# One row block of w2 brought in as seven SyncE transfers and seventeen one-row GpSimd transfers

## The chip, the core and the metric

The kernel runs on one core of a Trainium2 chip. The metric is the time of one execution on the device in microseconds (us). Before the change the median of three runs is 344.36 us (344.31 to 344.41).

## What is computed

One decoding step for two sequences: an attention block with 32 heads and a cache of 4096 positions, beside a small feed-forward block, mixed by a gate. All tensors are bf16.

```python
x = A_x                                                 # 2 x 1 x 512
g = sigmoid((x * gate_w).sum(-1, keepdims=True))
q = (x @ wq)                                            # 512 x 4096, 32 heads of 128
p = softmax(einsum("bhqd,bhkd->bhqk", q, k_cache) * 128 ** -0.5)
a = einsum("bhqk,bhkd->bhqd", p, v_cache) as (2, 1, 4096) @ wo
b = relu(x @ w1) @ w2                                   # w1 512 x 1376, w2 1376 x 512
out = g * a + (1 - g) * b
```

The two caches are 64 MB each as the kernel reads them (2 x 32 x 4096 x 128 values of two bytes); with the weights the kernel reads 145.46 MB.

## The kernel before, in words

The kernel is written out by hand for five engines. Every instruction is put on a list of its engine by a call such as `pe(...)`, `dve(...)`, `sp(...)` or `pool(...)`. A call may name a marker that it raises (`signal`), markers of other engines that it waits for (`waits`), and transfer semaphores that it waits for (`dwaits`). `_Prog.emit` turns these into semaphore waits, in the order of the lists. A transfer's completion adds 16 to its semaphore.

All large inputs are issued by SyncE (SP) into one hardware queue, in this order: w1 and wq (lines 267 and 268), K in ten pieces (line 272), V in nine pieces (line 282), wo in two (lines 283 and 284), and w2 in six (lines 285 and 290). A K or V piece is issued when the buffer that it overwrites is free: `kv` holds five places of 4 MB.

- K stage: for each of 64 pieces VectorE turns K by transposes of 32 x 32 blocks (line 386) and TensorE multiplies it with padded queries (lines 197 and 407).
- Softmax (lines 413 to 432) is done once over all scores. The exponentials are laid out for the V stage by `spread(j)` (lines 444 to 448), in four copies of 32 partitions: two on GpSimd, one on VectorE, one on ScalarE. They raise `pt_{j}_0` to `pt_{j}_3`.
- V stage: nine jobs. `v_unit(j)` multiplies the weights with one V unit (line 461), `v_extract` (lines 467 and 471) picks out the diagonal blocks, and `o_gather` (line 486) collects the heads.
- The end: `project` multiplies with wo (line 508), `ffn_f(r)` multiplies the hidden row block r with w2's row block r (line 516), `wo_sum` adds wo's four partial sums into the same PSUM bank (line 540), and `ffn_last` (lines 202 and 208) does the last blocks. The program's order on TensorE there is: project, ffn_f(10), wo_sum, ffn_f(0) to ffn_f(7), half of ffn_f(8), ffn_last. Four copies (lines 579 and 581) bring the result to SBUF, and two transfers of one row each (line 293, from SyncE and ScalarE) take it out.

w2 lies in `kt`, the buffer of the turned K, over the exponentials that `spread` reads, so its transfers wait for the last spread (`pt_8_0` to `pt_8_3`). w2 has 1376 rows. Rows 0 to 1279 are laid out with ten consecutive rows on each partition, `w2[:, 0..9, :]`, and come as the column ranges w2b, w2c, w2d, w2e and w2f (768, 320, 64, 64 and 64 KB). The last 96 rows do not fill 128 partitions. Row block 10 therefore takes rows 1248 to 1375, one row of 512 values (1 KB) on each partition, and the hidden values that would count rows 1248 to 1279 twice are set to zero (line 379). This block is the transfer w2a, 128 KB, semaphore `w2a`, and `ffn_f(10, first=True)` waits for it at its first matmul:

```python
sp(lambda e: e.dma_start(w2[:, 10, :], B_w2[1248:1376, :]).then_inc(sem["w2a"], 16),
   waits=[f"pt_8_{hq}" for hq in range(4)])
...
dw = {10: [(sem["w2a"], 16)], 0: [(sem["w2b"], 16)], 6: [(sem["w2c"], 16)]}.get(r, [])
```

The five other pieces of w2 follow w2a in SyncE's list. GpSimd issues no transfer at all. ScalarE issues three small ones: x (two rows of 1 KB), gate_w (one row) and one row of the output. The first K and V stages bear on the change only through the queue that they fill; markers, engines and lines named above are all that the change and the steps below touch.

Of the kernel before, what the change touches and what calls it, by code (L numbers as in the profile page):

```python
# [85 lines left out]
def bass_gated_mix__gqa_block_cached__dense_activation_relu__decode_kernel(  # L86
# [54 lines left out]
    w1 = flat[:, 0:2752].bitcast(dt.bfloat16)  # L141
    E = flat[:, 0:2048].bitcast(dt.bfloat16)
    ET = flat[:, 4096:6144].bitcast(dt.bfloat16)
    w2f = flat[:, 0:2816].bitcast(dt.bfloat16)
    w2 = w2f.rearrange("p (r n) -> p r n", n=512)
# [8 lines left out]
    def psf(p0, p1, c0, n):  # L154
        return PSF[p0:p1, c0:c0 + n]
# [15 lines left out]

    for e in ("pe", "dve", "act", "pool"):
        P.sems[e] = nc.alloc_semaphore(e + "_ev")
    names = ["x", "gw", "wq", "w1", "wo0", "wo1", "w2a", "w2b", "w2c", "w2d", "w2e", "w2f", "out"]
    sem = {n: nc.alloc_semaphore("sem_" + n) for n in names}
    sem_k = [nc.alloc_semaphore(f"sem_k{s}") for s in range(3)]
    sem_v = [nc.alloc_semaphore(f"sem_v{s}") for s in range(4)]
# [10 lines left out]
    def adder(engine):  # L188
        def add(fn, waits=(), signal=None, dwaits=()):
            P.add(engine, fn, waits=[marker(w) for w in waits], signal=marker(signal) if signal else None, dwaits=dwaits)  # L190
        return add

    pool, dve, act, pe, sp = (adder(e) for e in ("pool", "dve", "act", "pe", "sp"))
# [12 lines left out]
    def held_at(e, out, lhsT, rhs, g, last):  # L206
# [9 lines left out]
         waits=["c_i16z"], signal="c_i16")  # L216
# [5 lines left out]
         waits=["c_i32z"], signal="c_i32")  # L222
# [6 lines left out]
         waits=["c_s4z"], signal="c_s4")  # L229
# [39 lines left out]
    for g, (u, halves) in enumerate(segments):  # L269
# [3 lines left out]
           waits=([f"kt_{last_of[g - 3]}"] if g >= 3 else ["pe_qr1"] if g == 2 else []))  # L273
    for j, (u, hf) in enumerate(jobs):
# [7 lines left out]
        sp(lambda e, dst=dst, src=src, s=s: e.dma_start(dst, src).then_inc(sem_v[s], 16), waits=[w])  # L282
    sp(lambda e: e.dma_start(wo_sb[:, 0:12288], wo_in[:, 0:12288]).then_inc(sem["wo0"], 16), waits=["pe_v_2"])
    sp(lambda e: e.dma_start(wo_sb[:, 12288:16384], wo_in[:, 12288:16384]).then_inc(sem["wo1"], 16))
    sp(lambda e: e.dma_start(w2[:, 10, :], B_w2[1248:1376, :]).then_inc(sem["w2a"], 16),
       waits=[f"pt_8_{hq}" for hq in range(4)])


    for name, c0, c1 in (("w2b", 0, 3072), ("w2c", 3072, 4352), ("w2d", 4608, 4864), ("w2e", 4352, 4608), ("w2f", 4864, 5120)):
# [145 lines left out]
    def spread(j):  # L435
        u, hf = jobs[j]
        f0, n = (2 * u, 2) if hf is None else (2 * u + hf, 1)
        src = ET.rearrange("p (k f e) -> p f k e", f=16, e=2)
        for hq in range(4):
            args = dict(out=ptm[32 * hq:32 * hq + 32, j % 2, 0:128 * n, hq, :].rearrange("p (f k) e -> p f k e", f=n),  # L440
                        in_=src[32 * hq:32 * hq + 32, f0:f0 + n])
            waits = ["dve_et3", "c_ptm"] + ([f"pe_v_{j - 2}"] if j >= 2 else [])
            if hq < 2:
                pool(lambda e, args=args: e.tensor_copy(**args), waits=waits, signal=f"pt_{j}_{hq}")  # L444
            elif hq == 2:
                dve(lambda e, args=args: e.tensor_copy(**args), waits=waits, signal=f"pt_{j}_{hq}")
            else:
                act(lambda e, args=args: e.activation(func=ACT.Copy, **args), waits=waits, signal=f"pt_{j}_{hq}")  # L448

    def v_unit(j):  # L450
        u, hf = jobs[j]
        at = region[:, u % 2, :] if hf is None else kv[:, (4, 2)[hf], :]
        rows = at.rearrange("p (m c d) -> p m c d", c=4, d=128)
        n = 64 if hf is None else 32
        for m in range(n):
            t = m % 4
            waits, dwaits = [], []
            if m == 0:
                waits = [f"pt_{j}_{hq}" for hq in range(4)] + ([f"dve_y{j - 2}"] if j >= 2 else [])
                dwaits = [(sem_v[u % 2], 16 * (u // 2 + 1)) if hf is None else (sem_v[2 + hf], 16)]  # L460
            pe(lambda e, m=m, t=t: e.matmul(  # L461
                psf(32 * t, 32 * t + 32, V_B[j % 2] * BANK, 512), lhsT=ptm[:, j % 2, 4 * m:4 * m + 4, :, :],
                rhs=rows[:, m], start=(m < 4), stop=(m >= n - 4), tile_position=(0, 32 * t)),
               waits=waits, dwaits=dwaits, signal=(f"pe_v_{j}" if m == n - 1 else None))

    def v_extract(u):
        dve(lambda e: e.tensor_tensor(out=Y.rearrange("p (c d) -> p c d", c=4),  # L467
                                      in0=psf(0, 128, V_B[u % 2] * BANK, 512).rearrange("p (c d) -> p c d", c=4),
                                      in1=maskc[:, :].unsqueeze(2).to_broadcast([128, 4, 128]), op=ALU.mult),
            waits=[f"pe_v_{u}", "dve_maskc"] + ([f"dve_x{u - 1}"] if u else []), signal=f"dve_y{u}")  # L470
        dve(lambda e: e.tensor_reduce(out=X2[:, u, :], in_=Y.rearrange("p (c d) -> p d c", c=4), axis=AX.X, op=ALU.add),  # L471
            waits=[f"dve_y{u}"], signal=f"dve_x{u}")
# [10 lines left out]
    def o_gather(b, js, start, stop):  # L483
        for j in js:
            u, first, last = jobs[j][0] % 4, start and j == js[0], stop and j == js[-1]
            pe(lambda e, u=u, j=j, first=first, last=last: e.matmul(  # L486
                psf(0, 32, O_C0, 128), lhsT=selx[:, 24 - 8 * u:56 - 8 * u], rhs=X2[:, j, :], start=first, stop=last),
               waits=[f"dve_x{j}"] + (["dve_rinv", "dve_selx"] if first else []) + (["dve_O0"] if b else []),
               signal=(f"pe_O{b}" if last else None))
        if not stop:  # L490
            return
        dve(lambda v, b=b: v.tensor_scalar(out=O_sb[:, b, :], in0=psf(0, 32, O_C0, 128), scalar1=rinv[:, b:b + 1],
                                           scalar2=gb[0:32, b:b + 1], op0=ALU.mult, op1=ALU.mult),
            waits=[f"pe_O{b}", "dve_rinv", "dve_g"], signal=f"dve_O{b}")
        for dq in range(4):
            pe(lambda e, dq=dq, b=b: e.matmul(psf(0, 128, R_C0 + 32 * b, 32), lhsT=s4[:, dq, :], rhs=O_sb[:, b, 32 * dq:32 * dq + 32],
                                              start=(dq == 0), stop=(dq == 3), tile_position=(0, 0)),
               waits=([f"dve_O{b}", "c_s4"] if dq == 0 else []), signal=(f"pe_R{b}" if dq == 3 else None))
        dve(lambda v, b=b: v.tensor_copy(out=oW[:, :, b], in_=psf(0, 128, R_C0 + 32 * b, 32)), waits=[f"pe_R{b}"], signal=f"dve_oW{b}")

    def fin(g):
        return psf(32 * g, 32 * g + 2, FIN_B * BANK, 128)

    def project():
        for r in range(32):
            dw = [(sem["wo0"], 16)] if r == 0 else [(sem["wo1"], 16)] if r == 24 else []
            t = r % 4
            pe(lambda e, r=r, t=t: e.matmul(psf(32 * t, 32 * t + 2, WO_B * BANK, 512), lhsT=oW[:, r, :], rhs=wo_sb[:, 512 * r:512 * r + 512],  # L508
                                            start=(r < 4), stop=(r >= 28), tile_position=(0, 32 * t)),
               dwaits=dw, waits=(["dve_oW0", "dve_oW1", "dve_z"] if r == 0 else []), signal=("pe_wo" if r == 31 else None))  # L510
        dve(lambda v: v.tensor_copy(out=YW, in_=psf(0, 128, WO_B * BANK, 512)), waits=["pe_wo"], signal="dve_yw")

    def ffn_f(r, first=False, groups=4):
        dw = {10: [(sem["w2a"], 16)], 0: [(sem["w2b"], 16)], 6: [(sem["w2c"], 16)]}.get(r, [])
        for g in range(groups):
            pe(lambda e, g=g: e.matmul(fin(g), lhsT=hT[:, r, :], rhs=w2[:, r, 128 * g:128 * g + 128],
                                       start=first, stop=False, tile_position=(0, 32 * g)),
               dwaits=(dw if g == 0 else []), waits=(["dve_h0", "dve_h1", "c_h10", "dve_z"] if first and g == 0 else []))
# [40 lines left out]
    for j in range(9):  # L559
        if j < 8:  # L560
            spread(j + 1)
        v_unit(j)
        v_extract(j)
        if j == 4:
            o_gather(0, [0, 1, 3], True, False)
        if j == 5:
            o_gather(0, [4], False, True)
    o_gather(1, [2, 5, 6, 7, 8], True, True)
    project()
    ffn_f(10, first=True)  # L570
    wo_sum()
    for r in range(8):
        ffn_f(r)
    ffn_f(8, groups=2)
    ffn_last()
    for c in range(4):
# [38 lines left out]
```

## Time and profile before

| what | value |
|---|---|
| runs, median (lowest to highest) | 344.36 us (344.31 to 344.41) |
| profiled execution, first to last instruction (span) | 342.9 us |
| difference of the median and the span | 1.46 us |
| DMA engines' share of the chain that ended last | 68% |
| read from HBM, mean rate over the span | 145.46 MB, 424 GB/s |
| share of SyncE's and ScalarE's hardware queues q1 and q10 | 98.5%, 0.0% |
| busy: TensorE, VectorE, ScalarE, GpSimd | 58%, 52%, 7%, 6% |
| w2's six transfers, issue to landing | 30.4 to 32.3 us |
| last w2 transfer's issue, SyncE held | 8.84 us |

The span is that of one execution under the profiler; the runs' times also hold what lies outside of the first and last instruction, so only differences are carried from one to the other. A busy share is an average over stages: TensorE is busy 58% of the time and yet waits for transfers at the end of the kernel. "Issue to landing" is the time from the instruction that starts a transfer to its completion, so it holds the time for which the transfer stands in the queue behind others. The trace also keeps one record for each DMA packet (queue, start, duration, bytes) and one for each semaphore increment of a transfer; a transfer that runs on several of the 16 DMA engines raises its semaphore once from each of them.

### The profile page before, as it was taken

What the parts mean: (1) busy time and instruction counts of PE and PEld (TensorE: products, weight loads), DVE (VectorE), ACT (ScalarE), POOL (GpSimd) and SP (SyncE); (2) the same over time, 40 slices, a digit from 0 to 9 for tenths busy, and PEclk for the clock granted to TensorE, in tenths of its full rate; (3) what the DMA queues carried; (4) which work ended last, traced back from release to release, by engine and by line L of the source; (5) the groups of instructions that cost most, each with busy time, mean ns of one, the idle gap of its engine ahead of it and who ended that gap; (6) DMA issues with size and microseconds to landing.
All of it is one profiled execution on the core that took longest, in us unless ns stands there. A gap on an engine that the chain in (4) does not pass through costs nothing.

```text
span 342.9 us, 2540 instructions
## 1 busy us (share of the span) xinstructions
PE 197.8 (58%) x1228; PEld 54.3 (16%) x972; DVE 178.5 (52%) x127; ACT 23.1 (7%) x71; POOL 19.9 (6%) x36
## 2 busy tenths in 40 slices
PE   0177329799969799699799337220706043150656
PEld 0141001111111111111111013100303011020231
DVE  2239059899789899698999562220100103020121
ACT  1040000000000000000000240000000000000000
POOL 8000000000000000000000040110100101000000
PEclk9999959989999999989999858755656756565787
DMA  8998989899998999999999999999999999998996
GB/s 348 428 489 369 482 375 482 382 474 413 438 489 367 429 443 466 392 459 390 475 420 436 461 390 420 445 466 413 443 413 445 428 428 443 413 468 382 440 401 239
DMA packets 4196, 145.61 MB, mean 425 GB/s; under 512 B 469, under 2 KB 986, under 8 KB 1242
## 3 DMA queue, kind: packets, MB, share of 16 engines
q1 hardware_dynamic: 4178, 145.46, 98.5%
q8 instruction: 8, 0.13, 0.2%
q14 instruction: 2, 0.02, 0.0%
q10 hardware_dynamic: 8, 0.00, 0.0%
HBM read 145.46 MB, written 0.00 MB: 424 GB/s over the span
## 4 chain that ended last, share of the span: by engine, by line
DMA 68%; DVE 15%; PE 13%; ACT 1%; issue 1%; POOL 0%; SPq 0%; DVEq 0%
DMA kv<-in_A_k_cache_dram 31%; DMA kv<-in_A_v_cache_dram 23%; DVE kt L386 13%; DMA kt<-in_B_w_dram 9%; PE PS L461 6%; DMA kv<-in_A_wq_dram 4%; PE PS L407 3%; PE PS L197 3%; ACT kt L428 1%; PE PS L333 1%; DVE mpad L413 1%; DVE kt L471 1%; POOL ptm L444 0%; DVE qbuf L467 0%; DVE kt L432 0%
## 5 line engine op out<-in xcount | busy, mean ns | idle before, releaser
L386 DVE STREAM_TRANSPOSE kt<-kv 128x2048 f32<-128x2048 f32 x64 | 141.2, 2274 | 22.4 <-DMA kv<-in_A_k_cache_dram 22.3
L407 PE MATMUL PS<-kt,qbuf 128*128 128x512 bf16 x256 | 105.7, 413 | 31.8 <-DVE kt L386 26.3
L197 PE MATMUL PS<-kt,qbuf 128*128 128x512 bf16 x256 | 105.1, 411 | 0.0
L461 PE MATMUL PS<-kv,ptm 128*32 128x512 bf16 x512 | 46.5, 541 | 79.0 <-DMA kv<-in_A_v_cache_dram 76.0
L467 DVE TENSOR_TENSOR qbuf<-PS,maskc 128x512 f32<-128x512 f32 x9 | 6.2, 692 | 109.0 <-PE PS L461 109.0
L407 PEld LDWEIGHTS PS<-kt,qbuf 128*128 128x128 bf16 x256 | 25.5, 100 | 139.9 <-DVE kt L386 72.7
L461 PEld LDWEIGHTS PS<-kv,ptm 128*32 128x32 bf16 x512 | 19.0, 129 | 105.1 <-issue 98.6
L444 POOL COPY ptm<-kt 32x512 bf16<-32x512 bf16 (+1 forms) x18 | 11.5, 638 | 268.7 <-DVE rsum L475 175.6
L360 ACT ACTIVATE qbuf<-PS 32x8 bf16<-32x8 bf16 x40 | 7.9, 196 | 134.2 <-PE PS L197 132.7
L448 ACT ACTIVATE ptm<-kt 32x512 bf16<-32x512 bf16 (+1 forms) x9 | 5.3, 603 | 100.1 <-PE PS L461 98.7
L471 DVE TENSOR_REDUCE kt<-qbuf 128x128 f32<-128x512 f32 x9 | 9.3, 1028 | 0.3
L428 ACT ACTIVATE kt<-PS,negm 128x512 bf16<-128x512 f32 x8 | 5.4, 696 | 30.4 <-DVE negm L424 30.4
L333 PE MATMUL PS<-kv,xTw 128*32 128x512 bf16 x32 | 3.6, 629 | 5.9 <-DMA kv<-in_A_wq_dram 5.9
L478 PE MATMUL PS<-rsum,sell 128*32 128x1 f32 x4 | 0.4, 196 | 10.1 <-DVE rsum L475 10.1
L432 DVE STREAM_TRANSPOSE kt<-kt 128x1024 bf16<-128x1024 bf16 x4 | 5.0, 1245 | 1.7 <-ACT kt L428 1.4
L348 DVE CAST qrow<-PS 128x256 bf16<-128x256 f32 x2 | 2.4, 1396 | 6.4 <-PE PS L333 6.4
L508 PE MATMUL PS<-kv,oW 128*2 128x512 bf16 x32 | 3.4, 590 | 1.4 <-DMA kv<-in_A_wo_dram 1.4
L300 PE MATMUL PS<-ident,x_sb 3*128 3x3 bf16 x4 | 0.3, 166 | 6.2 <-DMA x_sb<-in_gate_w_dram 6.2
L486 PE MATMUL PS<-kt,selx 128*32 128x128 f32 x18 | 3.4, 328 | 0.3 <-DVE kt L471 0.3
L303 DVE COPY xT<-PS 128x12 bf16<-128x12 bf16 x1 | 0.2, 169 | 6.5 <-PE PS L300 6.5
L230 POOL MEMSET ptm<- 128x4096 bf16 x1 | 3.5, 3501 | 0.0
L413 DVE TENSOR_REDUCE mpad<-PS 128x1 f32<-128x2048 f32 x1 | 2.3, 2290 | 2.1 <-PE PS L197 2.1
(64 smaller groups left out, 44.2 us busy)
## 6 DMA issues: line engine op xcount, KB each, us to landing
kv<-in_A_k_cache_dram SPq DMA_DIRECT2D x4, 4096.0 KB, 31.6
kv<-in_A_v_cache_dram SPq DMA_DIRECT2D x2, 4096.0 KB, 27.0
kv<-in_A_wq_dram SPq DMA_DIRECT2D x1, 4096.0 KB, 15.0
kv<-in_A_wo_dram SPq DMA_DIRECT2D x1, 3072.0 KB, 29.3
kt<-in_B_w_dram SPq DMA_DIRECT2D x1, 1376.0 KB, 5.8
kv<-in_A_wo_dram SPq DMA_DIRECT2D x1, 1024.0 KB, 31.3
kt<-in_B_w_dram SPq DMA_DIRECT2D x1, 768.0 KB, 31.9
kt<-in_B_w_dram SPq DMA_DIRECT2D x1, 320.0 KB, 32.3
```

What stands on the lines that cost most here:

```text
L197: return e.add_instruction(mybir.InstMatmult(start_tensor_calc=start, stop_tensor_calc=stop, tile_size=(128, 128), tile_position=(0, 0), l ...
L333: pe(lambda e, n=n, t=t: e.matmul(psf(32 * (n % 4), 32 * (n % 4) + 32, (QR_B + n // 4) * BANK, 512), lhsT=xTw[:, t, :], rhs=wq_sb[:, t, n ...
L360: act(lambda a, hq=hq: a.activation(out=qbuf[32 * hq:32 * hq + 32, g % 2, :, :, 32 + 32 * hq], in_=cols[32 * hq:32 * hq + 32, u4 // 2, 2 * ...
L386: dve(lambda v: v.transpose(out=dst, in_=pairs[:, h, 64 * rr:64 * rr + 64]), waits=([f"pe_sc_{i - NKT}"] if i >= NKT else ["pe_h"] if i == ...
L407: return e.matmul(args[0], lhsT=args[1], rhs=args[2], start=first, stop=last)
L413: dve(lambda v: v.tensor_reduce(out=mpad[:, 0:1], in_=psf(0, 128, 0, 2048), axis=AX.X, op=ALU.max), waits=["pe_sc_63", "c_mpad"], signal=" ...
L428: act(lambda a, bk=bk, e2=e2: a.activation(out=blocks[:, bk, :, 16 * e2:16 * e2 + 16], in_=psf(0, 128, bk * BANK, 512).rearrange("p (r n) ...
L444: pool(lambda e, args=args: e.tensor_copy(**args), waits=waits, signal=f"pt_{j}_{hq}")
L448: act(lambda e, args=args: e.activation(func=ACT.Copy, **args), waits=waits, signal=f"pt_{j}_{hq}")
L461: pe(lambda e, m=m, t=t: e.matmul(psf(32 * t, 32 * t + 32, V_B[j % 2] * BANK, 512), lhsT=ptm[:, j % 2, 4 * m:4 * m + 4, :, :], rhs=rows[:, ...
L467: dve(lambda e: e.tensor_tensor(out=Y.rearrange("p (c d) -> p c d", c=4), in0=psf(0, 128, V_B[u % 2] * BANK, 512).rearrange("p (c d) -> p ...
L471: dve(lambda e: e.tensor_reduce(out=X2[:, u, :], in_=Y.rearrange("p (c d) -> p d c", c=4), axis=AX.X, op=ALU.add), waits=[f"dve_y{u}"], si ...
```

## The change

Row block 10 of w2 no longer comes as one transfer of 128 rows. SyncE brings partitions 0 to 110 as seven transfers of 15, 14, 13, 9, 7, 5 and 48 rows, in the place of w2a and with its waits on the first of them, all on semaphore `w2a`. GpSimd brings partitions 111 to 127 as seventeen transfers of one row each on a new semaphore `w2s`; the first waits for the same four markers. The calls to the GpSimd list stand behind the last `spread`. `ffn_f(10)` waits for 7 x 16 = 112 on `w2a` and 17 x 16 = 272 on `w2s`.

```diff
-    names = ["x", "gw", "wq", "w1", "wo0", "wo1", "w2a", "w2b", "w2c", "w2d", "w2e", "w2f", "out"]
+    names = ["x", "gw", "wq", "w1", "wo0", "wo1", "w2a", "w2b", "w2c", "w2d", "w2e", "w2f", "w2s", "out"]
...
-    sp(lambda e: e.dma_start(w2[:, 10, :], B_w2[1248:1376, :]).then_inc(sem["w2a"], 16),
-       waits=[f"pt_8_{hq}" for hq in range(4)])
+    ready = [f"pt_8_{hq}" for hq in range(4)]
+    few, p0 = [], 0
+    for n in (15, 14, 13, 9, 7, 5, 48):
+        few.append((p0, p0 + n))
+        p0 += n
+    for p0, p1 in few:
+        sp(lambda e, p0=p0, p1=p1: e.dma_start(w2[p0:p1, 10, :], B_w2[1248 + p0:1248 + p1, :]).then_inc(sem["w2a"], 16),
+           waits=ready if p0 == 0 else [])
...
+    def w2_single():
+        for p in range(111, 128):
+            pool(lambda g, p=p: g.dma_start(w2[p:p + 1, 10, :], B_w2[1248 + p:1249 + p, :]).then_inc(sem["w2s"], 16), waits=ready if p == 111 else [])
...
-        dw = {10: [(sem["w2a"], 16)], 0: [(sem["w2b"], 16)], 6: [(sem["w2c"], 16)]}.get(r, [])
+        dw = {10: [(sem["w2a"], 112), (sem["w2s"], 272)], 0: [(sem["w2b"], 16)], 6: [(sem["w2c"], 16)]}.get(r, [])
...
+    w2_single()
     o_gather(1, [2, 5, 6, 7, 8], True, True)
```

## The prediction

> **What bounds the kernel now.** I read the chain of waits first, then busy time in short stretches of the tail, then SyncE's and TensorE's timelines. The chain, from the last softmax-weight copy on:
>
> ```profile
> 306.97 0.28 DVE ptm L446
> ...
> 307.33 0.33 SPq L285
> ...
> 307.70 0.43 SPq L290
> ...
> 308.17 32.26 DMA kt<-in_B_w_dram
> ...
> 340.47 0.33 PE PS L516 x10
> 340.80 0.44 PE PS L208 x6
> ...
> 341.27 0.28 DVE out_sb L579
> ```
>
> Columns: start, duration, what. Transfers into kt (w2) end the kernel; after the last pieces of w2 only 0.8 us of matmul, a copy and the output's trip are left. These 32 us are not w2's own: it is 1.4 MB behind 8 MB of wo and V in one queue. The stretches of the tail (length, busy time of PE, PEld, DVE, ACT, POOL, clock, share of the 16 DMA engines busy, GB/s):
>
> ```profile
> 317.00:327.00 10.00, 5.40 (x64) 2.28 (x64) 1.71 (x2) 0.00 (x0) 0.00 (x0) 0.77 1.00 429
> ...
> 338.00:339.00 1.00, 0.54 (x9) 0.00 (x0) 0.52 (x1) 0.00 (x0) 0.00 (x0) 0.67 0.92 340
> 339.00:340.00 1.00, 0.75 (x32) 0.42 (x32) 0.17 (x1) 0.00 (x0) 0.00 (x0) 1.00 0.56 203
> 340.00:341.00 1.00, 0.69 (x26) 0.28 (x16) 0.08 (x1) 0.08 (x1) 0.00 (x0) 1.00 0.21 59
> ```
>
> Full until 338, then 0.92, 0.56, 0.21: the engines do not finish together. The trace's landing records (one per engine and transfer) say how unevenly. w2f, the last piece, lands between 339.09 and 339.64 on seven engines, at 340.31 on one, and between 340.78 and 340.97 on eight. Mean 340.17, last 340.97: perfect balance would be worth 0.80 us, and the end is set by the eight late engines alone. I followed packets (each starts within some 10 ns of its engine's last). An engine falls behind by about 1.5 us when a 16384-byte packet of the instruction queue q8 runs on it (eight in the span, the last at 331.8, each on another engine).
>
> **What is removed and added.** The same 128 rows of 1 KB come. Prices from the packet records: a 1024-byte packet 46 ns, a semaphore increment (a 4-byte packet) 9 ns. w2a is now 8 rows and one increment on each engine: 8 x 46 + 9 = 377 ns.
>
> How are odd numbers of rows spread? Rows of the trace: gate_w, one row, made one packet and one increment; x, two rows, two of each; 128 rows, 8 packets on each of 16 engines. I extend this: n rows below 16 go to n engines, one each, 48 rows three to each, always from the same first engine. The first five engines then get 9 rows and 7 increments, 9 x 46 + 7 x 9 = 477, **+0.10 us**; the next two 8 and 6, +0.05; two 7 and 5, -0.01; four 6 and 4, -0.07; then -0.12 and -0.18; the last 3 rows and one increment, 147, **-0.23 us**. [...]
>
> The seventeen single rows add 46 + 9 = 55 ns to each engine if they go round, one engine getting two. Bounds: 0.055, and with all increments on all engines (below) 0.20.
>
> Which engines are late? Only one can be named: the engine that carried gate_w, so the first, is among the seven early ones. Eight of the other fifteen are late. Best case, the eight late ones are the relieved ones and the last is the most relieved: -0.23 + 0.055 = -0.18 us. Worst, a late one is among the first five and gets two singles: +0.10 + 0.20 + 0.05 = +0.35. One late engine among the four loaded ones that remain is enough to move the end the loaded way, so I take +0.10 + 0.055 = **+0.15 us**.
>
> **SyncE's queue.** It issues 6 transfers more ahead of w2b to w2f.
>
> ```profile
> 307.33 0.33 SPq L285 DMA_DIRECT2D kt<-in_B_w_dram  x1
> 307.70 10.74 SPq L290 DMA_DIRECT2D kt<-in_B_w_dram  x5
> 341.61 0.32 SPq L293 DMA_DIRECT2D out_dram<-out_sb  x1
> ```
>
> An issue takes 0.43, yet five took 10.74: the fifth, w2f, held SyncE 8.84 us, until 318.4, right after V unit 6 landed (317.83). It was the tenth transfer in flight. If that is a limit of nine, the n-th of now sixteen gets in when the (n-9)-th has landed. V unit 6, its successor, wo0 and wo1 land at 317.8, 327.5, 334.9, 337.4. The sixth short transfer goes in at 317.8, the seventh at 327.5, w2b at 335, w2c at 337.5, and w2d, w2e, w2f by their own 0.45 each, to 339.3. x's first packet started 0.4 us after its issue ended, so w2f is in the engines by 339.7. The late ones need it after w2e, landing 340.79; they work on w2c at 339.7. Cost on the late engines **0**; the early ones run dry for about a microsecond, covered by their 1.3 to 1.9 us of lead. If the limit counts packets instead, I get w2f in at 336.7: 0 as well. Without that cover, w2f's 1 us would be the price.
>
> **GpSimd and the new wait.** The singles wait for the four copies of the last spread, ready at 307.24; nothing is behind them on GpSimd. TensorE's line 516 waits for all of them at row block 10, with everything to the end queued behind:
>
> ```profile
> 338.21 0.32 PE L516 MATMUL PS<-kt,hT 128*2 128x128 bf16 x4
> 339.23 0.40 PE L540 MATMUL PS<-qbuf,selw 128*2 128x128 f32 x8 [0.69 <-DVE qbuf L511]
> 339.65 0.51 PE L516 MATMUL PS<-kt,hT 128*2 128x128 bf16 x24
> 340.47 0.33 PE L516 MATMUL PS<-kt,hT 128*2 128x128 bf16 x10 [0.32 <-DMA kt<-in_B_w_dram]
> ```
>
> Blocks 10, the wo sum and r = 0 to 5 are 0.32 + 0.40 + 0.51 = 1.23 us and must be over at 340.43, when w2c lands: the singles are free until 339.2. The only small transfer that met a full queue, gate_w, landed 4.5 us after its issue ended (1.55 to 6.03): its row went behind some seven queued packets, then one packet of the big queue, then its increment. So the last issue may end at 334.7, or (334.7 - 307.3) / 17 = **1.6 us each**. No GpSimd issue is in the trace; ACT's two took 0.55 and 0.23, SyncE's 0.33 to 0.43, and SyncE's longest was 8.84 when blocked. Ends: 17 x 0.23 = 4 us, hidden; 17 x 8.84 = 150 us, absurdly late. The nearest row is a small issue on an engine's own queue, 0.55: done at 317, cost **0**. [...]
>
> **Sum.** +0.15 in the queues, 0 elsewhere. The profiled span is 342.9 and 1.46 below the median of the runs, 344.36; I keep that difference: 343.05 + 1.46 = **344.5 us**.
>
> **Rivals.**
> *All increments on all engines* (0.24). Every single row then puts 17 increments, not one, on each engine: 17 x 9 + 46 = 0.20, the end +0.30, 344.7. For: nothing in the trace; against: gate_w and x post one increment per engine used. [...] The turns would still suffice: 7 packets ahead and 18 turns make 25, and an engine has 28 large packets left before w2a.
> *The late engines are the relieved ones* (0.07): down to -0.18, 344.2.
> *GpSimd is too slow* (0.14, the slower side): from 1.6 us per issue on, each 0.1 us more adds 1.7 us; at 2 us the last is issued at 341.3, lands at about 342.8, and 2 us of matmuls follow where they now end at 341.24: some 348. At 1.65 to 1.75, 345.3 to 347. Against it: every issue row but the blocked one is under 0.6.
> *The change doesn't spread as meant* (0.07): singles all on one late engine cost 17 x 55 = 0.94 there, less its relief or plus its load, 345.1 to 345.4; the 63 rows of the six odd transfers piled on one engine would make (63 + 3 - 8) x 46 ns = 2.67 there, of which the lead of an early one (1.3 to 1.9) hides half or more: 345.2 to 345.7.
> *SyncE's slots starve the late engines* (0.05): up to 1 us, 344.9 to 345.4; decides if w2c or w2f comes over 1.1 us later than worked out.
> *Faster by over 0.7* (0.05): would need nearly all of the 0.80; five rows less are 0.23. Only instruction packets falling on other engines could do it.
>
> **Chances.** A measurement of this kernel can tell about 0.2%, 0.69 us. My forecast has 0.38; with the first two rivals, all within 0.69, same is 0.69. Slower: 0.14 + 0.07 + 0.05 = 0.26. Faster 0.05. The forecast's own range is 344.2 to 344.7; the range 344.1 to 345.6 takes in the queue bounds (-0.18, +0.35), the spread and the slot rivals, and leaves out most of GpSimd's 0.14 and the 0.05.
>
> **What would show it.** w2f's landing about 0.15 later and the chain still ending in kt; GpSimd's issues under 1.6 us each and done by 334; line 516's first four matmuls still at about 338.2. Wrong if these wait for GpSimd's transfers, or if the share of busy DMA falls below 1 before 338.

## The result and the profile after

Five runs of the changed kernel have a median of 345.80 us (345.49 to 346.10), five of the kernel before 344.31 (344.21 to 344.41): 1.49 us slower by the medians, ratio 1.0041, 95% interval 1.0027 to 1.0054. The prediction was 344.5 us, range 344.1 to 345.6. The profiled execution has a span of 344.2 us; 342.9 before. These 1.3 us are what the traces can account for; the other 0.2 lies outside of the spans or between executions, and no run explains it.

The chain of waits of the changed kernel still ends in kt, as before (start, duration, what):

```profile
308.92 32.69 DMA kt<-in_B_w_dram
...
341.65 0.33 PE PS L526 x10
341.98 0.54 PE PS L208 x6
...
342.55 0.28 DVE out_sb L590
```

Compare with the chain before: the matmuls that wait for w2c begin at 341.65 instead of 340.47, 1.18 us later, and what follows takes 0.10 us longer. So the loss is in the transfers ahead of them: w2f's last landing is at 342.25 instead of 340.97, and the span ends 1.97 us after it, where it ended 1.98 us after it before. The stretches of the tail show in what form (length, busy time of PE, PEld, DVE, ACT, POOL, clock, share of the DMA engines busy, GB/s). First the kernel before, from 336 to 338:

```profile
336.00:337.00 1.00, 1.00 (x16) 0.29 (x8) 0.00 (x0) 0.00 (x0) 0.00 (x0) 0.50 0.96 383
337.00:338.00 1.00, 1.00 (x16) 0.24 (x12) 0.00 (x0) 0.00 (x0) 0.00 (x0) 0.50 1.02 404
```

and the changed kernel:

```profile
336.00:337.00 1.00, 1.00 (x16) 0.43 (x12) 0.00 (x0) 0.00 (x0) 0.00 (x0) 0.50 1.10 330
337.00:338.00 1.00, 0.95 (x12) 0.02 (x3) 0.00 (x0) 0.00 (x0) 0.00 (x0) 0.50 1.03 302
338.00:339.00 1.00, 0.64 (x8) 0.10 (x8) 0.00 (x0) 0.00 (x0) 0.00 (x0) 0.50 0.95 319
339.00:340.00 1.00, 0.52 (x8) 0.09 (x4) 0.65 (x1) 0.00 (x0) 0.00 (x0) 0.97 0.86 321
340.00:341.00 1.00, 0.59 (x24) 0.30 (x28) 0.04 (x1) 0.00 (x0) 0.00 (x0) 1.00 0.64 222
341.00:342.00 1.00, 0.66 (x36) 0.32 (x26) 0.00 (x0) 0.00 (x0) 0.00 (x0) 1.00 0.17 49
```

The engines stay busy about a microsecond longer, and they move less while busy: 319 GB/s at a share of 0.95, where a share of 0.92 moved 340 before, and 302 GB/s at 1.03 in the stretch from 337 to 338, where the kernel before moved 404 at 1.02. Smaller packets alone lower the rate too (in the kernel before 8192 bytes take 313 ns on average, 1024 bytes 46 and 512 bytes 27: 26, 22 and 19 bytes for each ns), so the packet records have to be asked: the packets that start from 336 to 337 and from 337 to 338 take 1.10 and 1.03 us of each engine, and at the mean duration that each size has in the kernel before they would take 0.84 and 0.80. So the engines are not idle, their packets are slow. The table of queues has a new line:

```profile
DMA packets 4786, 145.61 MB, mean 423 GB/s; under 512 B 1076, under 2 KB 1576, under 8 KB 1832
## 3 DMA queue, kind: packets, MB, share of 16 engines
q1 hardware_dynamic: 4224, 145.44, 98.4%
...
q0 software_dynamic: 544, 0.02, 0.1%
```

GpSimd's seventeen rows made 544 packets, not 34. By the packet records these are 272 of 64 bytes and 272 increments: each row is cut into 16 pieces with 16 increments, and 544 packets on 16 engines are 34 on each. The busy share of that queue, 0.1%, looks harmless.

What did not happen is in the timeline of GpSimd, SyncE and TensorE:

```profile
306.36 8.25 POOL L458 DMA_DIRECT2D kt<-in_B_w_dram  x17 [1.77 <-issue]
308.45 17.79 SPq L296 DMA_DIRECT2D kt<-in_B_w_dram  x5
...
339.68 0.23 PE L526 MATMUL PS<-kt,hT 128*2 128x128 bf16 x4 [0.39 <-DMA kt<-in_B_w_dram]
340.10 0.40 PE L550 MATMUL PS<-qbuf,selw 128*2 128x128 f32 x8 [0.19 <-DVE qbuf L521]
340.81 0.51 PE L526 MATMUL PS<-kt,hT 128*2 128x128 bf16 x24 [0.31 <-DMA kt<-in_B_w_dram]
```

GpSimd issued all seventeen in 8.25 us. Row block 10's matmuls start 1.5 us later than before, at 339.68, but block 10 and the wo sum are over at 340.50, before w2b lets the next matmuls start at 340.81: the new wait costs nothing. Nor is it GpSimd's rows that block 10 waits for. By the landing records these are there at 338.83, and the last of SyncE's seven transfers at 339.63.

### The profile page after: what moved, and what is told of

Same layout as the page of the kernel before. It is cut to its first block, busy times and chain, and to the rows that moved or that the text cites. A ratio compares the mean times of both kernels' runs of the same rounds, so it can differ in the third digit from the quotient of the medians.

```text
span 344.2 us, 2565 instructions
## 1 busy us (share of the span) xinstructions
PE 196.9 (57%) x1228; PEld 53.9 (16%) x972; DVE 178.1 (52%) x127; ACT 23.1 (7%) x71; POOL 28.2 (8%) x53
## 4 chain that ended last, share of the span: by engine, by line
DMA 76%; DVE 11%; PE 11%; SPq 1%; issue 0%; DVEq 0%
DMA kv<-in_A_k_cache_dram 31%; DMA kv<-in_A_v_cache_dram 31%; DVE kt L392 10%; DMA kt<-in_B_w_dram 9%; PE PS L471 5%; DMA kv<-in_A_wq_dram 4%; PE PS L413 3%; PE PS L197 2%; PE PS L339 1%; SPq L291 1%; DVE kt L481 0%; DVE qbuf L477 0%; PE PS L208 0%; SPq L296 0%; SPq L267 0%
## 5 line engine op out<-in xcount | busy, mean ns | idle before, releaser
L471 PE MATMUL PS<-kv,ptm 128*32 128x512 bf16 x512 | 44.4, 520 | 81.7 <-DMA kv<-in_A_v_cache_dram 80.5
L471 PEld LDWEIGHTS PS<-kv,ptm 128*32 128x32 bf16 x512 | 18.3, 124 | 106.3 <-issue 100.8
L458 POOL DMA_DIRECT2D kt<-in_B_w_dram x17 | 8.3, 494 | 1.8 <-issue 1.8
```

The source lines that it names most:

```text
L458: pool(lambda g, p=p: g.dma_start(w2[p:p + 1, 10, :], B_w2[1248 + p:1249 + p, :]).then_inc(sem["w2s"], 16), waits=ready if p == 111 else [])
L471: pe(lambda e, m=m, t=t: e.matmul(psf(32 * t, 32 * t + 32, V_B[j % 2] * BANK, 512), lhsT=ptm[:, j % 2, 4 * m:4 * m + 4, :, :], rhs=rows[:, ...
```

## The experiments

Each number is the difference of the medians against the kernel before on the same chip; the ratio has its 95% interval. In every trace but that of the thirty-four rows the span ends 1.97 to 2.11 us after w2f's last landing, at granted clocks between 0.50 and 1.00 from 340 to 341, so TensorE's part in these differences is at most 0.14 us. `ready` stands for the four markers `pt_8_0` to `pt_8_3`. In "added" runs the block comes as before in one transfer of 128 rows, and the named transfers are added, into a spare tile that nothing reads; TensorE's block 10 waits for them too. The others bring the same 128 rows of the block by other transfers.

**First round: which half of the change costs?**

SyncE's half alone. 

> Row block 10 comes from SyncE alone: the same 15, 14, 13, 9, 7, 5 and 48 rows, then 16 and 1 row instead of GpSimd's seventeen transfers; each has a semaphore of its own. Theory A (the seventeen one-row transfers cost the time, because the changed kernel's trace shows 272 packets of 64 bytes and 272 increments on GpSimd's queue, 34 packets on each DMA engine): +0.1 to +0.4 us against the kernel before, from 8 more increments of 9 ns and up to 2 more rows of 46 ns on the loaded engines. Theory B (the uneven split of SyncE's transfers costs it): +1.0 us or more.

```diff
+    for i, n in enumerate((15, 14, 13, 9, 7, 5, 48, 16, 1)):
+        sp(lambda e, p0=p0, n=n, i=i: e.dma_start(w2[p0:p0 + n, 10, :], B_w2[1248 + p0:1248 + p0 + n, :]).then_inc(sem["w2a%d" % i], 16),
+           waits=ready if i == 0 else [])
+        p0 += n
```

Measured: +0.60 us, 1.0020 (1.0011 to 1.0029). Between the two theories: neither half is the whole.

GpSimd's half with an even split. 

> SyncE brings 112 rows in one transfer, evenly, and GpSimd the last 16 as sixteen one-row transfers. Theory A: +0.8 to +1.1 us (16/17 of the 0.96 us by which the last landing of the second piece of wo, which lies ahead of row block 10 in the queue, is later in the changed kernel's trace). Theory B: under +0.3 us.

```diff
+    sp(... w2[0:112, 10, :] ..., waits=ready)
...
+        pool(lambda e, p0=p0, n=n: e.dma_start(w2[p0:p0 + n, 10, :], B_w2[1248 + p0:1248 + p0 + n, :]).then_inc(sem["w2s"], 16),
+             waits=ready if i == 0 else [])     # p0 from 112, n = 1, sixteen times
```

Measured: +1.19 us, 1.0035 (1.0023 to 1.0048). Near theory A, and yet A was wrong, as the next two show.

The 16 rows in one GpSimd transfer. 

> SyncE brings 112 rows in one transfer and GpSimd the last 16 rows in a single transfer. Theory A (it is the number of one-row transfers): a sixteenth of the cost of sixteen, so within 0.1 us of the kernel before. Theory C (that GpSimd issues a transfer at all, a third queue beside the others, costs it): +0.7 us or more.

Measured: +0.50 us, 1.0017 (1.0008 to 1.0026). Neither A nor, quite, C. The code is the excerpt above with one transfer of n = 16.

The 16 rows from ScalarE, one by one. 

> SyncE brings 112 rows in one transfer and ScalarE the last 16 as sixteen one-row transfers. x and gate_w made one packet of 1024 bytes and one increment for each row on ScalarE's queue. Theory A (the many small packets on all engines cost): 16 x 55 ns on the first engine alone, which is among the early ones, so within 0.1 us of the kernel before. Theory D (many transfers on another queue cost, however few packets they make): +0.7 us or more.

Measured: +0.61 us, 1.0018 (1.0009 to 1.0027). A had said that nothing would be lost, D +0.7 or more; neither holds. The code is the excerpt above with the sixteen calls on ScalarE's list. All three kernels with 112 rows in one SyncE transfer lose at least half a microsecond, whatever brings the other 16 rows. Something in the 112-row transfer itself costs time, although by its packets it is cheaper than the 128-row transfer (7 x 46 + 9 = 331 ns on an engine instead of 377, an estimate from the prices of the packet records).

The packet records show what. In the kernel before, a packet of wo's second part (8192 bytes) takes 313 ns on average and one of w2b (6144 bytes) 242. In the run with one GpSimd transfer these are 328 and 277, and the slow ones run between 335.2 and 337.8, while SyncE's 112 rows are in flight (335.0 to 337.3). The 8192-byte packets stand ahead of the rows in every engine's queue, so an engine is slowed there by rows that *other* engines carry. New theory, P: a row that an engine writes to partitions which another engine serves in full transfers collides with that engine's packets. That each engine has partitions of its own in full transfers is a part of the theory: no record here names an engine or the partitions that it writes. The pair of runs in the third round tests whether it matters where the rows go.

**Second round: number of transfers, or whose partitions?**

Eight transfers of 16 neighbouring rows. 

> SyncE alone brings the block as eight transfers of 16 neighbouring rows. By the packet prices it is 8 x (46 + 9) = 440 ns on each engine instead of 377, +0.06 us. Theory P (rows that an engine writes to partitions which other engines write in full transfers collide with those engines' packets: in the trace with one GpSimd transfer the 8192- and 6144-byte packets that run while the rows are in flight took 7.2 us more in all, 0.45 us per engine): +0.5 us or more, and at least 0.2 us more than the same with rows eight apart. Theory N (the number of transfers and increments): the same as with rows eight apart, and no slow 8192-byte packets.

```diff
+    for j in range(8):
+        sp(lambda e, j=j: e.dma_start(w2[16 * j:16 * j + 16, 10, :], B_w2[1248 + 16 * j:1264 + 16 * j, :]).then_inc(sem["w2a"], 16),
+           waits=ready if j == 0 else [])
```

Measured: +0.83 us, 1.0024 (1.0015 to 1.0033).

Eight transfers of rows eight apart. 

> As the one before, but each transfer takes rows eight apart, so that its 16 rows are spread over all partitions. Number of transfers, packets and increments are the same. Theory P: +0.1 to +0.4 us, the excess of the 8192- and 6144-byte packets under half of that with neighbouring rows. Theory N: the same time as with neighbouring rows.

```diff
+        sp(lambda e, j=j: e.dma_start(w2[j::8, 10, :], B_w2[1248 + j:1376:8, :]).then_inc(sem["w2a"], 16), ...
```

Measured: +0.79 us, 1.0020 (1.0011 to 1.0029). Spreading the rows did not help as P had said it would; the slow packets cost nearly as much (10.7 us of engine time in all, 11.8 with neighbouring rows). P had been read too simply: which of the 128 rows fall on partitions that their engine writes in full transfers is shown for neither kernel, so that fewer packets would be slow here was the author's guess. Nor is N right by itself, since 8192-byte packets are slow in both.

Two transfers, full height. 

> SyncE brings the block as two transfers of all 128 partitions, 512 bytes of each row. By the packet prices 16 x 27 + 2 x 9 = 450 ns instead of 377, +0.07 us. Theory P: within 0.15 us of the kernel before, no slow packets. Theory F (any second transfer for this block costs the 0.5 us that the evenly split kernels showed): +0.4 us or more.

```diff
+    for j in range(2):
+        sp(lambda e, j=j: e.dma_start(w2[:, 10, 256 * j:256 * j + 256], B_w2[1248:1376, 256 * j:256 * j + 256]).then_inc(sem["w2a"], 16),
+           waits=ready if j == 0 else [])
```

Measured: +0.09 us, 1.0001 (0.9992 to 1.0009), as P and the packet prices (+0.07) say; the slow packets are few, not none (1.1 us of engine time, 0.4 before). Here, where each transfer covers all partitions, the second one costs no more than its packets.

The single rows, added. 

> The block comes as before in one SyncE transfer of 128 rows; GpSimd's seventeen one-row transfers are added and go to a spare tile, with TensorE waiting for them as in the change (17 KB more are read than needed). Two causes together (uneven ownership of partitions, and the small packets of the one-row transfers): the small packets alone cost 34 x 10 ns = 0.34 us to 0.7 us, so +0.3 to +0.8 us. If only SyncE's rows on other engines' partitions cost anything: under 0.2 us.

```diff
+    for p in range(111, 128):
+        pool(lambda g, p=p: g.dma_start(spare[p:p + 1, :], B_w2[1248 + p:1249 + p, :]).then_inc(sem["w2s"], 16), waits=ready if p == 111 else [])
```

Measured: +0.83 us, 1.0022 (1.0013 to 1.0031). Its stretches from 336 to 338 move 395 and 398 GB/s, nearly as before (383 and 404): hardly any collisions, only more work. The time is just above the +0.3 to +0.8 that was expected of two causes together. With SyncE's half, 0.60 + 0.83 = 1.43 us, near the change's 1.49.

**Third round: P and the single rows, each against its rival.**

The next two kernels differ in one number, 0 or 64, which the excerpt calls `base`:

```diff
+    for j in range(8):
+        at = base + 32 * (j // 4) + j % 4
+        sp(lambda e, at=at: e.dma_start(spare[at:at + 29:4, :], B_w2[1248 + at:1248 + at + 29:4, :]).then_inc(sem["w2a"], 16))
```

P's forecasts rest on an assumption of the author's, that the rows meet other engines' packets with 64 and not with 0; no run shows which partitions an engine writes. That a short transfer runs on as many engines as it has rows is shown for other numbers than 8: in SyncE's half alone those of 15, 14, 13, 9, 7 and 5 rows have as many landings.

> The block comes as before in one transfer; SyncE adds eight transfers of 8 rows to a spare tile ahead of w2b, partitions four apart from 0 (+j, and +32 for the last four). They run on the first eight DMA engines. [...] 8 x (46 + 9) = 0.44 us more on each of the eight engines. Theory P (collision with the engine that owns the partitions): +0.3 to +0.5 us, and the 8192- and 6144-byte packets as fast as before (excess under 1.5 us in all). Theory N (short transfers themselves disturb the others): excess of 4 us or more, the same as with the partitions 64 higher.

> [...] Theory P: excess of the 8192- and 6144-byte packets 4 us or more in all, and 0.1 to 0.5 us more than with the partitions from 0. Theory N: no difference between the two.

Measured: +0.81 us, 1.0024 (1.0015 to 1.0033) with the partitions from 0; +1.35 us, 1.0039 (1.0027 to 1.0052) with those from 64. Same number of transfers and rows: where they go costs 0.54 us, and 2.9 us of engine time in slow packets of 8192 bytes where there were none. The number also moves the rows that are read by 64, so the pair alone doesn't exclude the source; but the same rows are read in the kernel before and in the two transfers of full height, with no slow packet of 8192 bytes. The stretches from 336 to 338, first with the partitions from 0:

```profile
336.00:337.00 1.00, 1.00 (x12) 0.15 (x4) 0.00 (x0) 0.00 (x0) 0.00 (x0) 0.50 1.04 380
337.00:338.00 1.00, 0.55 (x12) 0.10 (x8) 0.00 (x0) 0.00 (x0) 0.00 (x0) 0.50 1.03 367
```

and with those from 64:

```profile
336.00:337.00 1.00, 0.96 (x12) 0.03 (x4) 0.00 (x0) 0.00 (x0) 0.00 (x0) 0.50 0.97 282
337.00:338.00 1.00, 0.04 (x4) 0.04 (x8) 0.00 (x0) 0.00 (x0) 0.00 (x0) 0.50 1.09 308
```

The last two columns are what to read: the engines are as busy, and move 282 and 308 GB/s instead of 380 and 367. At the mean durations of the kernel before, the packets that start in these stretches would take 0.71 and 0.80 us of each engine instead of 0.97 and 1.09 (from 0: 0.97 and 0.92 instead of 1.04 and 1.03). This is how a collision looks in these profiles: the busy share stays, the rate falls, and packets of one size take longer. Both theories hold a part, though: with the partitions from 0 no 8192-byte packet is slow, but 22 of w2b's are, by up to 0.40 us, and the run lost 0.81 where 0.44 was worked out.

> The block in one transfer as before, and thirty-four one-row GpSimd transfers to the spare tile, twice the number of the run with seventeen, which was 0.83 us slower than before. If each one-row transfer costs every engine the time of two small packets: +1.4 to +1.9 us. If it is GpSimd's queue being in use at all: +0.8 us again.

Measured: +3.79 us, 1.0111 (1.0097 to 1.0125): twice the number of the run with seventeen, but more than four times its cost. Both expectations miss, since a second effect comes in. Its chain of waits no longer runs through kt:

```profile
322.07 20.79 DMA spare<-in_B_w_dram
342.86 0.14 issue
342.99 0.27 PE PS L517 x3
343.27 0.43 PE PS L541 x8
343.69 0.95 PE PS L517 x34
```

TensorE stands until 342.86 for GpSimd's rows: here the wait decides, which in the change had 0.3 us to spare. The last pieces of w2 are late as well (w2f's last landing 343.26 instead of 340.97), so the wait is only a part of the 3.79 us.

> The block in one transfer as before, and the seventeen added one-row transfers of the spare tile issued by ScalarE instead of GpSimd. If the cost is the cutting of each row into 16 pieces with 16 increments on all engines: 17 x (46 + 9) = 0.94 us on the first engine alone, which is ahead of the late ones by more, so within 0.3 us of the kernel before. If it is the number of transfers: +0.8 us.

Measured: +0.04 us, 1.0001 (0.9992 to 1.0010), as expected. Its table of queues:

```profile
q1 hardware_dynamic: 4178, 145.46, 98.5%
q8 instruction: 8, 0.13, 0.2%
q10 hardware_dynamic: 42, 0.02, 0.0%
```

q10 has 34 packets more than before, two for a row, where GpSimd's queue had 544 for the same seventeen rows. The number of transfers is not the cost. What differs is how many packets there are, and perhaps where: GpSimd's rows make 34 for each engine, late ones too, while ScalarE's 34 were taken to run all on the engine that carried gate_w's one row, which is early. No run names the engine. The result fits the cutting as the cause, but the run doesn't part it from another cost of GpSimd's path.

**Fourth round: what was still open.**

Four added transfers of 8 partitions with 2 KB each, on partitions from 0: as many bytes as in the run there with eight, which lost 0.81 us where its packets explain 0.44, in half as many transfers (the 0.38 that the expectation calls unexplained is from 0.82). 

> [...] If a short transfer costs its engine a stall beside its packets: about half of the unexplained 0.38, in all +0.45 to +0.65 us. If the bytes count: +0.8 us again. If four in a row are too few for a stall: +0.3 to +0.4 us.

```diff
+    for j in range(4):
+        at = 32 * (j // 2) + j % 2
+        sp(lambda e, at=at: e.dma_start(spare[at:at + 29:4, :]..., B_w2[1248:1264, :]...).then_inc(sem["w2a"], 16))   # 8 partitions x 2 KB
```

Measured: +0.22 us, 1.0007 (0.9998 to 1.0016), no slow packets of either size. The bytes were the same as in the run with eight transfers, so the bytes by themselves are not the cost. Two things changed, though: half as many transfers, and packets of 2 KB instead of 1 KB (from the same 16 rows each time). That eight short transfers cause a stall and four don't is the likely reading, not shown. The time is below all three numbers that were expected, and its interval takes in no change at all.

> The block in one transfer as before, and one added GpSimd transfer of 16 rows to the spare tile. If the count of GpSimd's one-row transfers makes their cost (+0.83 us for seventeen): within 0.1 us of the kernel before. If the first use of GpSimd's queue costs: +0.4 us or more.

Measured: +0.30 us, 1.0008 (1.0000 to 1.0017). More than 0.1 and less than 0.4: not decided, except that one transfer costs less than seventeen. Its 32 packets are 16 of 1024 bytes and 16 increments, so these rows were not cut up. Part of the cost is again a collision, with larger packets: of the 25 packets of 65536 bytes that start between 309 and 313.05, around the rows (310.7 to 313.5), 22 take longer than any that starts there in the kernel before, up to 2.60 us instead of 2.42 to 2.43, in all 1.6 us of engine time.

> The seventeen added one-row GpSimd transfers to the spare tile are issued in the middle of the V stage, near 250 us, instead of at its end. If they cost the DMA engines' time (34 packets each, the queue is full there too): +0.4 to +0.9 us again, wherever they stand. If the cost is that they stand beside the last pieces or that TensorE waits for them: within 0.2 us of the kernel before.

```diff
+        if j == 3:
+            for p in range(111, 128):
+                pool(lambda g, p=p: g.dma_start(spare[p:p + 1, :], ...).then_inc(sem["w2s"], 16),
+                     waits=[f"pt_4_{hq}" for hq in range(4)] if p == 111 else [])
```

Measured: +0.68 us, 1.0020 (1.0011 to 1.0029). Their packets ran between 231.7 and 304.9, far from the tail, and landed 30 us before TensorE needs them. So neither the wait nor the place beside the last pieces is the cost: the rows cost engine time where they stand.

The slow packets, by the packet records: the sum over all packets that took over 15 ns more than their size takes alone (310 ns for 8192 bytes, 234 for 6144), in us of engine time; sixteen of these are one microsecond of all engines.

| kernel | 8192 bytes | 6144 bytes | time against before |
|---|---|---|---|
| before | 0.0 | 0.4 | |
| two transfers of 128 half rows | 0.0 | 1.1 | +0.09 |
| seventeen rows added, from ScalarE | 0.6 | 0.6 | +0.04 |
| one GpSimd transfer of 16 rows added | 0.0 | 0.4 | +0.30 |
| seventeen single rows added, near 250 us | 0.0 | 0.4 | +0.68 |
| four short transfers added, partitions from 0 | 0.0 | 0.3 | +0.22 |
| seventeen single rows added | 0.2 | 0.8 | +0.83 |
| eight short transfers added, partitions from 0 | 0.0 | 4.2 | +0.81 |
| thirty-four single rows added | 0.7 | 5.3 | +3.79 |
| 112 rows, and 16 single ones from GpSimd | 2.2 | 4.8 | +1.19 |
| 112 rows, and 16 in one GpSimd transfer | 2.0 | 5.2 | +0.50 |
| 112 rows, and 16 single ones from ScalarE | 2.8 | 5.1 | +0.61 |
| SyncE's half alone | 2.7 | 6.4 | +0.60 |
| eight transfers of 16 rows, eight apart | 1.8 | 8.9 | +0.79 |
| eight transfers of 16 neighbouring rows | 2.9 | 8.9 | +0.83 |
| eight short transfers added, partitions from 64 | 2.9 | 9.0 | +1.35 |
| the change | 3.3 | 9.8 | +1.49 |

The slow packets don't give the time by themselves: they count every engine, and the late ones alone set the end (in the kernel before w2f lands between 339.09 and 340.97, and the last of these counts). Nor does every small packet collide. GpSimd's pieces of 64 bytes (11 ns each) hardly slow the others, with 0.2 and 0.8 us for seventeen rows.

No version beat the kernel before.

## Why the prediction was wrong

The forecast was +0.15 us in the queues and 0 elsewhere. The place was right, the tail of the transfer queue, and both terms of the queue were too small.

- **SyncE's split: "+0.10 us" on the most loaded engines; measured +0.60** (with the last 17 rows on SyncE too). The step that failed is the price: each packet was priced by its own duration, 46 and 9 ns, as if it could not change another one's. The rows of short transfers lengthen packets that other engines carry (shown by 8192-byte packets that take 328 ns instead of 313 with 112 rows and one GpSimd transfer, though they stand ahead of the rows in their own queue), and how much depends on the partitions (shown by the pair that differs in where the rows go, 0.54 us); that it is the partitions of those other engines is theory P, which no run shows. Strings of short transfers add something more (eight on the partitions from 0 cost 0.81 us where their packets explain 0.44); a stall is the likely reading, not shown. The spread of the rows itself was extended rightly: the landings of the 15-, 14-, 13-, 9-, 7- and 5-row transfers in SyncE's half alone are that many, beside one record of each that comes 0.13 to 0.18 us after its issue ended.
- **Which engines are late: left open; one of the first five was taken to be late.** From those landings, an engine missing in the next shorter transfer can be told: in that run the late ones are the sixth, the seventh and the tenth to the fifteenth, none of the first five. If they are the same in the change, it relieves six of the eight late engines and loads two by 0.05 us; by packet prices alone it would have been worth next to nothing. The split looks like a relief of late engines, and the collisions undo it.
- **The single rows: "+0.055", with a rival of 0.20; measured +0.83.** The rival, all increments on all engines, was right in kind: the change's trace has 272 increments for the seventeen rows, 16 for each. No run shows its 0.20, since the row was priced as one packet of 1024 bytes, from gate_w's transfer, which ScalarE issued, and on GpSimd's path it became sixteen of 64. That is 34 x 10 = 0.34 us for each engine by the packets' durations, and 0.37 us by the mean landing of w2f in the run with the rows added (340.54 against 340.17). The last landing there is 0.59 us later, the span 0.70 (after the landing, the granted clock from 340 to 341 is 0.50 instead of 1.00, which fits the other 0.11), the time 0.83. Why the last engine loses more than the mean is not settled.
- **SyncE's slots: cost 0, right; the reading of the limit, wrong.** Nine transfers in flight is not the limit: fourteen were issued by 309.8, the fifteenth, w2e, was held 7.59 us until V unit 6 had all but landed, and w2f 8.74 us more, until 326.2. With SyncE's half alone sixteen are in flight before SyncE is held. So no one number of transfers is the limit; the other reading, a limit on packets, was not tried. The queue did not run dry: from 317 to 339 the share of busy DMA is 0.95 to 1.10 in the stretches of the trace (334 to 336 taken as one, 0.95 against 0.99 before).
- **GpSimd's issues: right.** 0.48 us each after the first, where the nearest rows had 0.23 to 0.55 and 1.6 was allowed. The turns were foreseen in kind, not in number: 18 turns on each engine were counted for all increments on all engines, and the cut rows took 34. Issued by 314.6, the packets ran until 337.6, and the wait was spared by 0.3 us; with thirty-four rows it was not.
- **The test named in the prediction** would have caught it: w2f's landing was to be 0.15 us later; it is 1.28 us later (342.25 against 340.97). Line 516's first four matmuls (line 526 after the change) were to start still at about 338.2; they start at 339.68, behind SyncE's rows and not GpSimd's.
- **The rivals.** None had the mechanism. Two had times near 345.8: GpSimd too slow (345.3 to 347), but its issues took 0.48 us and not 1.65 to 1.75, and rows piled on one engine (345.2 to 345.7), but the landings show SyncE's rows spread as meant.

## What to carry to other kernels

Where transfers bound a kernel, price a new transfer not by its bytes and packets alone: ask which partitions it writes (here 0.81 us from 0 and 1.35 us from 64), and into how many packets its path cuts it (here 544 from GpSimd and 34 from ScalarE for the same seventeen rows). A transfer of part of the partitions beside full ones can cost more than its own packets: here 1.35 us where these were worked out at 0.44. To see it, read the busy share of DMA and the rate side by side in the same stretch. A share that falls, here from 0.92 to 0.21 between 338 and 341 before the change, is engines that have run out of packets. A share that stays while the rate falls, here 1.03 at 302 GB/s after 1.02 at 404, is slow or small packets; and packets of one size that take longer than in the kernel before, here 312 ns on average instead of 242 for 6144 bytes, tell a collision from small packets.

## What the hardware showed that was not expected

- A one-row transfer of 1 KB became 16 packets of 64 bytes and 16 increments from GpSimd, and one packet and one increment from ScalarE: seventeen of them cost 0.83 us and 0.04 us (an estimate from gate_w's row has ScalarE's all on one engine, which is early).
- The same eight short transfers cost 0.81 us with the partitions from 0 and 1.35 us with the partitions 64 higher.
- Increments of short transfers in a row lag behind their rows: in SyncE's half alone the first landings of the first four transfers are 335.43, 335.70, 335.96 and 336.19, a quarter of a microsecond apart, though a row and an increment take 55 ns. In the change the last landing of SyncE's rows of the block is at 339.63, 1.8 us after its last row's packet ended (337.84). That the stall behind eight short transfers comes from this lag is likely, but it was not tried by itself.
